# Tables, projections and u in the order of the source: a pipeline over half groups, row tiles of 32 and taps of two terms

## The chip, the core and the metric

The kernel runs on one core of a Trainium2 chip. The metric is the device time of one execution in microseconds (us). Three executions of the kernel before took 1042.09 to 1048.74 us, with a median of 1042.39 us. The core has five engines that each work through a list of instructions of their own in order: PE (matrix multiplication, with weight loads PEld beside it), DVE (vector operations), ACT (activation functions and copies), POOL (vector operations of a second kind) and SP, which here only issues DMAs. An instruction starts when it is first in its engine's list and the semaphores it waits for are there.

## The reference

Two independent computations on inputs of 2048 rows and 576 columns are written side by side into one output of 2048 by 1152.

- Part A is attention. `qkv = x @ wqkv`, 32 heads of 18 columns, a causal window of 256 keys, softmax, and the output projection `@ wo`.
- Part B is a long convolution. For each of 576 channels a kernel of 2048 taps is made from 128 complex modes, `K[d, l] = Re sum_n C[d,n] * exp(dt_d * A[d,n] * l) * dt_d * B[d,n]`. Then `y = u * K` as a causal convolution by transforms of length 4096, plus `u * Dskip`.

## The kernel before

The work runs in three stages.

**Stage 1** makes everything that the second half needs, as three streams that are interleaved in the source by a helper, `merge`, in proportion to their lengths:

- `proj` (line 182) loads x and wqkv, finds a scale for each from their largest absolute values (`amax`, `pow2_scale`), splits both into two float16 halves, and multiplies. `mm14` (line 164) is one group of 14 matmuls of 512 or 288 columns into one PSUM tile. For each of four column chunks of 512 there are nine such groups for q and k, whose results are split again into two float16 halves (`qst`, lines 236 and 237) and stored to DRAM, and four pairs of groups for v (line 248).
- `tables` (line 430) makes the taps of the convolution. The 576 channels come in 36 half groups of 16, and two half groups `c` make a group `q`. The tap at position `l = 64 * a + m` is a product of a coarse factor (over `a`) and a fine one (over `m`). `factors(q)` (line 352) makes the coarse factors of a group: a small matmul, a fraction (ACT line 324, DVE lines 325 and 326), two sines (ACT line 331), then six POOL operations (lines 362 to 373). `products(c)` (line 377) multiplies out two tiles of 128x1024 per half group on POOL (line 384). `phases(c)` and `qtable(c)` make the fine factors: a matmul, a fraction, two sines into PSUM and four DVE products into the tile `Q` (lines 404 to 407). Exponentials for four half groups at a time come from `exps_ab` and `exps_q` (two and eight ACT operations on line 331 from small matmuls on line 314); exponentials and sines need different tables in ACT, so each such block stands between two table loads. `taps(c)` (line 411) sums over the 128 modes: for 4 channels times 4 strips there are four matmuls each (two product tiles, two signs) of 128x32 weights and 64 columns. The profile has two records for each float32 matmul, so one half group has 128 records on line 422.
- `s1_u` (line 470) makes the first step of the transform of u: 32 point transforms over strips of 32 partitions, by a weight of 128x128 that holds the same 32x32 cosine (or sine) block four times on its diagonal (`w1`). Results go to the DRAM tile `gx`.

The order of the instructions of this stage on each engine is set by the framework's scheduler, which reorders the traced instructions by its own cost estimates.

**Stage 2**, `s1_k` (line 479), does for the taps `K` what `s1_u` does for u, and stores them into `gk`. It needs all taps. Beside it the setup of the attention runs (`att_setup`, line 588), with memory fills of the buffers for q and k (lines 601, 603, 604).

**Stage 3** is the attention with the rest of the convolution woven in (`attention`, `conv`), and then the output projection. Its order is already that of the source: it is traced under `manual_schedule()`.

Tile pools set how far the streams can run ahead: a tile with `bufs` buffers can be written again only when all users of the one `bufs` before it are done.

## Time and profile before

| what | value |
|---|---|
| executions, median of 3 | 1042.39 us |
| profiled execution | 1041.77 us |
| its span from first to last instruction | 1040.1 us |
| PE busy | 842.3 us (81%) |
| DVE busy | 703.1 us (68%) |
| POOL busy | 593.5 us (57%) |
| ACT busy | 569.9 us (55%) |
| HBM traffic | 89.12 MB read, 61.01 MB written |

A row of the timeline has the start, the duration, the engine, the line, the operation, the tile written and the tiles read, and in brackets the idle time of the engine before it with what ended the wait. A row of groups has the count after the `x`, then the total busy time and the mean duration in ns, then the idle time before these instructions. A row of stretches has the busy time of PE, PEld, DVE, ACT and POOL, the number of instructions in brackets, the granted clock of PE, the busy share of the DMA engines and GB/s. Busy time is a share of the whole span only as an average; the stretches below show that the three stages are limited by different things.

### The profile page before, as it was taken

Reading aid. Unit: us, or ns where it says so; the run is one execution under the profiler, and the core shown is the slowest. Engines: PE = TensorE matmul, PEld = TensorE weight load, DVE = VectorE, ACT = ScalarE, POOL = GpSimd, SP = SyncE. Lnnn points to the kernel's source line nnn. Section 1 sums busy time; section 2 is a strip of 40 time slices with the busy share of each in tenths; the row PEclk is TensorE's granted clock in tenths of the full one; section 3 lists DMA queues with packets and bytes.
Section 4 is the critical chain, followed back from the end, with each engine's and each line's share of the span. In section 5 each row is a group of like instructions: output and inputs, shape, how many; then the busy total and the mean of one; then the engine's idle time right before and its main releaser. Section 6 shows DMA issues by size and latency. Waiting matters only on the chain.

```text
span 1040.1 us, 26776 instructions
## 1 busy us (share of the span) xinstructions
PE 842.3 (81%) x10332; PEld 443.0 (43%) x10332; DVE 703.1 (68%) x1805; ACT 569.9 (55%) x883; POOL 593.5 (57%) x714
## 2 busy tenths in 40 slices
PE   1433998989799899865788888878888999987787
PEld 0212456446457457532343333333333444433345
DVE  2879374674765675464867788878878676767554
ACT  1784466666666666331266565556666565634470
POOL 0036495674676596301266776757776757664780
PEclk9956899999999999898899999999999999989999
DMA  9655544443454333587144465464544563579863
GB/s 271 182 169 154 133 108 102 113 99 84 124 114 106 79 89 92 135 257 218 48 126 136 130 209 157 147 177 129 158 124 146 144 184 113 152 175 240 222 185 124
DMA packets 155911, 152.27 MB, mean 146 GB/s; under 512 B 36856, under 2 KB 134392, under 8 KB 155592
## 3 DMA queue, kind: packets, MB, share of 16 engines
q1 hardware_dynamic: 148152, 131.98, 46.8%
q0 software_dynamic: 6128, 14.60, 5.5%
q10 hardware_dynamic: 1504, 3.99, 1.4%
q8 instruction: 81, 1.33, 0.6%
q14 instruction: 46, 0.38, 0.1%
HBM read 89.12 MB, written 61.01 MB: 144 GB/s over the span
## 4 chain that ended last, share of the span: by engine, by line
PE 40%; DVE 21%; DMA 12%; issue 10%; ACT 7%; POOL 7%; SPq 2%; DVEq 0%; ACTq 0%; POOLq 0%
PE pp L172 11%; PE r L641 4%; PE kp L422 4%; PE r L505 4%; PE po L705 4%; PE r L908 4%; DVE jk L648 3%; PE pp L466 3%; POOL P L693 3%; PE x L314 2%; DMA gk<-g 2%; PE ST L682 2%; DVE qb L632 2%; ACT P L684 2%; PE r L513 2%
## 5 line engine op out<-in xcount | busy, mean ns | idle before, releaser
L648 DVE CUSTOM_DVE_ANT_0 jk<-r,bias 128x288 f32<-128x288 f32 (+7 forms) x512 | 198.4, 433 | 96.8 <-PE r L641 95.9
L684 ACT ACTIVATE P<-ST,esc 128x1024 f32<-128x1024 f32 (+1 forms) x192 | 201.8, 1058 | 94.5 <-PE ST L682 93.5
L693 POOL TENSOR_SCALAR_AFFINE_SELECT P<-P 128x512 f32<-128x512 f32 x240 | 171.1, 741 | 107.0 <-ACT P L684 104.6
L384 POOL TENSOR_TENSOR m<-A,tr 128x1024 f32<-128x1024 f32 x72 | 145.6, 2045 | 86.8 <-PE kp L422 79.6
L641 PE MATMUL r<-K,qb 128*64 128x288 f16 (+7 forms) x1024 | 130.4, 297 | 38.3 <-DVE qb L632 11.2
L541 POOL TENSOR_TENSOR Y<-t,t 64x288 f32<-64x288 f32 x64 | 52.9, 826 | 119.8 <-DMA tk<-gk 59.8
L705 PE MATMUL po<-P,V 128*32 128x256 f32 (+2 forms) x1408 | 100.6, 397 | 16.9 <-ACT osb L713 8.1
L641 PEld LDWEIGHTS <-qb 128*64 128x64 f16 x1024 | 60.1, 109 | 121.3 <-issue 67.3
L422 PE MATMUL kp<-Q,m 128*32 128x64 f32 x4608 | 80.6, 224 | 16.5 <-issue 6.1
L422 PEld LDWEIGHTS kp<-Q,m 128*32 128x32 f32 x4608 | 70.4, 112 | 38.8 <-issue 26.6
L466 PE MATMUL pp<-ut,w 128*128 128x288 f32 x128 | 47.8, 506 | 42.6 <-DMA ut<-in_u_dram 25.4
L682 PE MATMUL ST<-Q,K 64*128 64x384 f16 (+2 forms) x704 | 73.8, 281 | 3.0 <-DMA Q<-mt 2.9
L325 DVE TENSOR_TENSOR k<-x,k 128x512 f32<-128x512 f32 (+1 forms) x54 | 33.9, 638 | 39.1 <-ACT k L324 39.0
L237 DVE SCALAR_TENSOR_TENSOR qst<-pp,qst 128x512 f16<-128x512 f32 x36 | 24.7, 685 | 50.6 <-ACT qst L236 42.4
L705 PEld LDWEIGHTS po<-P,V 128*32 128x32 f32 x1408 | 35.8, 110 | 51.4 <-issue 26.4
L542 POOL TENSOR_TENSOR Y<-t,t 64x288 f32<-64x288 f32 x64 | 54.4, 851 | 3.8
L172 PE MATMUL pp<-xh,wh 128*128 128x512 f16 x180 | 48.3, 391 | 9.4 <-DVE xh L229 6.5
L128 ACT ACTIVATE g<-pp 128x288 f32<-128x288 f32 (+1 forms) x84 | 34.1, 447 | 37.9 <-DMA gk<-g 20.0
L362 POOL TENSOR_TENSOR tr<-tr,mab 128x768 f32<-128x768 f32 x18 | 34.7, 1929 | 31.1 <-ACT tr L331 31.1
L466 PEld LDWEIGHTS pp<-ut,w 128*128 128x128 f32 x128 | 26.5, 227 | 58.2 <-ACT g L128 17.5
L172 PEld LDWEIGHTS <-wh 128*128 128x128 f16 x324 | 31.6, 99 | 45.7 <-issue 12.4
L505 PE MATMUL r<-tx,w 128*64 128x288 f32 x256 | 41.2, 439 | 10.7 <-DMA tx<-gx 9.5
(173 smaller groups left out, 1755.4 us busy)
## 6 DMA issues: line engine op xcount, KB each, us to landing
gx<-g SPq DMA_DIRECT2D x32, 288.0 KB
qd<-qst SPq DMA_DIRECT2D x72, 128.0 KB
gk<-g SPq DMA_DIRECT2D x16, 576.0 KB
tx<-gx SPq DMA_DIRECT2D x16, 576.0 KB
tk<-gk SPq DMA_DIRECT2D x16, 576.0 KB
h<-ho SPq DMA_DIRECT2D x16, 576.0 KB
raw<-in_xT_dram SPq DMA_DIRECT2D x16, 512.0 KB
Q<-qd SPq DMA_DIRECT2D x32, 216.0 KB
```

What stands on the lines that cost most here:

```text
L172: self.nc.tensor.matmul(ps, u, v, start=(i == 0), stop=(i == len(ops) - 1))
L384: self.nc.gpsimd.tensor_tensor(m, A[:, ch, a0:a0 + 8].unsqueeze(3).to_broadcast(sh), tr[:, ch, part, 0:8].unsqueeze(2).to_broadcast(sh), o ...
L422: nc.tensor.matmul(kp[32 * st:32 * st + 32, c % 2 * JJ2 + j, :], m[:, ch, a0:a0 + 32], Q[:, ch, term % 2, :], start=(term == 0), stop=(ter ...
L466: nc.tensor.matmul(ps, self.w1[:, part, :], src[:, o:o + k], start=True, stop=True)
L505: nc.tensor.matmul(ps[64 * par:64 * par + 64], w2[:, par, 64 * part:64 * part + 64], t[:, 2 * hs:2 * hs + 2, par, :], start=True, stop=True)
L542: nc.gpsimd.tensor_tensor(Y[par][64:128], t1[sl, 1], t2[sl, 1], op=OP.add)
L641: nc.tensor.matmul(ps[64 * b:64 * b + 64, :n], self.qb[:, b, t, :], d["K"][:, b, k0:k0 + n], start=True, stop=True, skip_group_check=True)
L648: nc.vector.tensor_tensor_reduce(out=jk[:, :n], in0=ps[:, :n], in1=self.bias[:, 288 - n:], scale=1.0, scalar=-3e38, op0=OP.add, op1=OP.max ...
L682: nc.tensor.matmul(ps[:, u, o:o + n], d["K"][h, jp, k0:k0 + 128], d["Q"][h, jp, q0:q0 + n], start=True, stop=True, skip_group_check=True)
L684: nc.scalar.activation(pt[:, 2 * jp:2 * jp + 2, lo:hi], ps[:, :, lo:hi], AF.Exp, scale=self.esc)
L693: nc.gpsimd.affine_select(v, v, pattern=[[0, 4], [sg, 128]], compare_op=OP.is_ge, fill=0.0, base=-1 if far else 0, channel_multiplier=-sg)
L705: nc.tensor.matmul(self.po[32 * j:32 * j + 32, t0 * 128:t1 * 128], V[:, kb * 76 + 19 * j:kb * 76 + 19 * j + 32], pt[:, j, o:o + (t1 - t0) ...
```

## The change

Six edits go together.

1. The second `merge` of stage 1 is traced under `manual_schedule()`. On every engine its instructions now stand in the order in which the source emits them. The first, shorter `merge` (16 units of `proj`, 20 of `tables`, 4 of `s1_u`) is still scheduled by the framework.
2. `tables` is written as a pipeline over half groups. In iteration `c` stand: the sum of the two product tiles of `c`, the phases of `c + 2`, the sines and `Q` of `c + 1`, the products of `c + 1`, the first step of the factors of the next group, the taps of `c`, the rest of the factors, and after every fourth the block of exponentials.
3. Taps have two terms. A new step, `sums`, adds the two product tiles on DVE (128x1024), and the taps need two matmuls where they needed four. The pool of the products is split into one with two buffers and one with one.
4. `s1` uses row tiles of 32: the weight is 32x64 (cosine beside sine), and each of the four strips is multiplied by itself into 64 PSUM partitions. `gx` and `gk` are laid out with the strip as an index, each store becomes four of 64 partitions where two of 128 partitions stood, `s1_k` has 16 steps of 4 rows where 8 of 8 rows stood, and `conv` loads `tx` and `tk` in two halves each.
5. The loads of x for the projections and of u are issued one chunk earlier.
6. Three pairs of fills with zero in the attention's setup (line 603) are left out.

```diff
 def proj:
+        load(0)
         for c in range(4):
...
             for hf in range(2):
-                t = self.p["raw"].tile([128, 5, 256], F32, name="raw")
-                self.load_rows(t, a["xT"], slice(c * 512 + hf * 256, c * 512 + hf * 256 + 256))
+                t = raws.pop(0)
...
+                if m == 1 and c < 3:
+                    load(c + 1)

 def products:
-            m = self.p["P"].tile(sh, F32, name="m%d" % part)
+            m = self.p["P%d" % part].tile(sh, F32, name="m%d" % part)
+    def sums(self, c):
+        r = self.P[c]
+        self.nc.vector.tensor_tensor(r[0], r[0], r[1], op=OP.add)
+        self.P[c] = r[0].rearrange("p c a b -> p c (a b)")

 def taps:
         for j in range(JJ2):
-            for term in range(4):
-                m = (m1, m2)[term // 2]
-                a0 = term % 2 * 32
+            for term in range(2):
                 for st in range(4):
                     ch = st * JJ2 + j
-                    nc.tensor.matmul(kp[32 * st:32 * st + 32, c % 2 * JJ2 + j, :], m[:, ch, a0:a0 + 32],
-                                     Q[:, ch, term % 2, :], start=(term == 0), stop=(term == 3), skip_group_check=True)
+                    nc.tensor.matmul(kp[32 * st:32 * st + 32, c % 2 * JJ2 + j, :], P[:, ch, 32 * term:32 * term + 32],
+                                     Q[:, ch, term, :], start=(term == 0), stop=(term == 1), skip_group_check=True)

 def tables:
-        for c in range(n):
-            if c % 2 == 0 and c // 2 + 1 < NQ:
-                yield from self.factors(c // 2 + 1)
-            if c + 1 < n:
-                self.phases(c + 1)
-                yield
-            yield from self.qtable(c)
-            yield
-            if c % 4 == 3 and c + 1 < n:
-                if c + 5 < n:
-                    yield from self.exps_ab(c // 4 + 2)
-                yield from self.exps_q(c // 4 + 1)
-            if c:
-                yield from self.taps(c - 1)
-            if c + 1 < n:
-                self.products(c + 1)
-        yield from self.taps(n - 1)
+        for c in range(-1, n):
+            if c >= 0:
+                self.sums(c)
+            if c + 2 < n:
+                self.phases(c + 2)
+                yield
+            if c + 1 < n:
+                yield from self.qtable(c + 1)
+                if c >= 0:
+                    self.products(c + 1)
+                yield
+            fa = self.factors(c // 2 + 1) if c % 2 == 0 and c + 2 < n else iter(())
+            if next(fa, 0) is None:
+                yield
+            if c >= 0:
+                yield from self.taps(c)
+            yield from fa
+            if (c + 1) % 4 == 3 and c + 2 < n:
+                if c + 6 < n:
+                    yield from self.exps_ab((c + 1) // 4 + 2)
+                yield from self.exps_q((c + 1) // 4 + 1)

 def s1:
+        st = [self.p["s1s"].tile([128, n], F32, name="g%d" % e) for e in range(2)]
+        for o in range(0, n, k):
+            ps = [self.p[pp].tile([128, 512], F32, name="pp")[:, :k] for _ in range(2)]
+            for q in range(4):
+                r, h = slice(32 * q, 32 * q + 32), 64 * (q % 2)
+                nc.tensor.matmul(ps[q // 2][h:h + 64], self.w1[r], src[r, o:o + k], start=True, stop=True,
+                                 skip_group_check=True)
+            for e in range(2):
+                self.evac(st[e][:, o:o + k], ps[e])
+        for q in range(4):
+            h = 64 * (q % 2)
+            nc.sync.dma_start(g[l0:l0 + nl, q].rearrange("l p j -> p l j"),
+                              st[q // 2][h:h + 64].rearrange("p (l j) -> p l j", j=144))

 def s1_k:
-        for b in range(8):
-            self.s1(kf[:, b * 1152:(b + 1) * 1152], self.gk, 8 * b, 8, "s1p")
+        for b in range(16):
+            self.s1(kf[:, b * 576:(b + 1) * 576], self.gk, 4 * b, 4, "s1p")

 def conv:
-                nc.sync.dma_start(t[nm], g.rearrange("a l (s f) j -> (a l) s f j", s=4)[:, :, 2 * fp:2 * fp + 2, :])
+                for e in range(2):
+                    f0 = 32 * e + 2 * fp
+                    nc.sync.dma_start(t[nm][64 * e:64 * e + 64], g[:, :, f0:f0 + 2])

 def att_setup:
-                nc.vector.memset(d["K"][h:h + 32], 0.0)

 def build:
-                                 ("mg", 4), ("fr", 2), ("Q", 2), ("P", 2)):
+                                 ("mg", 4), ("fr", 2), ("Q", 2), ("P0", 2), ("P1", 1)):
-                    merge((proj, 56), (tables, 304), (s1u, 12))
+                    with self.tc.manual_schedule():
+                        merge((proj, 56), (tables, 304), (s1u, 12))
-                    self.pool(e1, "s1p", 3, PSUM)
+                    self.pool(e1, "s1p", 4, PSUM)
```

38 lines of the change are left out of this document (19 added, 19 removed).

## The prediction

> **What bounds the kernel now.** I read the stretches first, to see which of the three stages the change touches and what each costs.
>
> ```profile
> 0.00:106.00 106.00, 36.83 (x339) 19.45 (x340) 73.94 (x82) 56.89 (x71) 27.51 (x26) 0.79 0.67 190
> 106.00:428.00 322.00, 297.69 (x5510) 184.15 (x5510) 191.45 (x284) 198.12 (x355) 210.73 (x168) 0.98 0.44 105
> 428.00:479.00 51.00, 36.74 (x108) 18.02 (x100) 30.03 (x29) 17.16 (x37) 2.40 (x1) 0.94 0.76 223
> 479.00:1041.00 562.00, 471.08 (x4386) 221.41 (x4386) 407.67 (x1412) 297.71 (x421) 352.88 (x520) 0.97 0.55 155
> ```
>
> Stage 1 runs to 428 us. From 106 us on, when the first projection starts, PE is busy in 298 of 322 us, DVE, ACT and POOL in 191 to 211. So PE sets the pace there, and the scheduler keeps it fed. Stage 2 (51 us) has the DMA engines at 0.76. Stage 3 (562 us) is touched only through how two tiles are loaded.
>
> Next the groups of stage 1 and single pieces of the timeline:
>
> ```profile
> L384 POOL TENSOR_TENSOR m<-A,tr 128x1024 f32<-128x1024 f32 x72 | 145.6, 2045 | 86.8 <-PE kp L422 79.6 <-issue 7.2
> L331 ACT ACTIVATE mg<-x 128x512 f32<-128x512 f32 x72 | 40.1, 599 | 8.8 <-PE x L314 8.3
> L325 DVE TENSOR_TENSOR k<-x,k 128x512 f32<-128x512 f32 x36 | 24.6, 682 | 2.7 <-ACT k L324 2.6
> L404 DVE TENSOR_TENSOR Q<-cs,mg 128x512 f32<-128x512 f32 x36 | 24.6, 684 | 3.0 <-ACT cs L331 3.0
> L261 DVE TENSOR_TENSOR res<-nA_re,al 96x2304 f32<-96x2304 f32 x1 | 2.5, 2547 | 0.0
> ...
> 300.23 1.03 PE L172 MATMUL pp<-xl,wh 128*128 128x512 f16 x4
> 301.18 1.99 PE L422 MATMUL kp<-Q,m 128*32 128x64 f32 x128
> ```
>
> One half group's taps take PE 1.99 us. Products are a slack engine's work: POOL idled 79.6 us before them, waiting for the taps that still read the old buffers.
>
> **The change, part by part.** *Taps of two terms* remove half of 1.99 us for each of the some 34 half groups after 106 us: 34 us of PE. *The sums* come to DVE: 2304 columns of two SBUF inputs took 2547 ns, so 1024 take 1.13 us, 34 x 1.13 = 38 us. DVE goes from 191 to about 230 of 322 us if nothing disturbs it. *Row tiles* can shorten PE by up to half of each pass over u, if the four strips run side by side. Attention's row tiles bear on that:
>
> ```profile
> 709.76 0.39 PE L682 MATMUL ST<-Q,K 64*128 64x384 f16 x4
> 710.08 0.50 PE L641 MATMUL r<-K,qb 128*64 128x288 f16 x4
> ```
>
> Four matmuls of 384 columns on two row halves took 0.32 us until the next started. In the fence above, the float16 group starts four of 512 columns in 0.95 us (300.23 to 301.18), 0.18 us per 384: one after another, four would need 0.71 us. So two row tiles do run side by side. By loads alone PE falls from 298 to about 255 us, and the stage ought to shrink.
>
> **But the new order decides what replaces PE.** In the manual order each engine keeps the source's order, so the waits can be walked through. I do this for a period of four half groups, the distance between two blocks of exponentials. These are the period's marks before (table loads of ACT) and one complete passage through the factors:
>
> ```profile
> 153.35 1.28 ACT L331 ACT_TABLE_LOAD   x1
> 169.59 1.28 ACT L331 ACT_TABLE_LOAD   x1 [0.18 <-DVE k L325]
> ...
> 388.44 1.28 ACT L331 ACT_TABLE_LOAD   x1
> ...
> 269.48 0.56 DVE L325 TENSOR_TENSOR k<-x,k 128x384 f32<-128x384 f32 x1
> 270.07 0.36 DVE L326 TENSOR_SCALAR ab<-k 128x384 int32<-128x384 int32 x1
> 270.13 0.52 ACT L331 ACTIVATE tr<-k 128x384 f32<-128x384 f32 x1 [7.18 <-DVE k L325]
> 270.56 0.60 ACT L331 ACTIVATE tr<-ab,halfpi 128x384 f32<-128x384 f32 x1
> 271.30 1.81 POOL L362 TENSOR_TENSOR tr<-tr,mab 128x768 f32<-128x768 f32 x1 [3.44 <-ACT tr L331]
> 276.21 3.86 POOL L384 TENSOR_TENSOR m<-A,tr 128x1024 f32<-128x1024 f32 x2
> ...
> 306.32 0.58 ACT L331 ACTIVATE sn<-k 128x512 f32<-128x512 f32 x1
> 306.84 0.67 ACT L331 ACTIVATE cs<-ab,halfpi 128x512 f32<-128x512 f32 x1
> ...
> 195.89 0.87 ACT L331 ACTIVATE mab<-x 128x384 f32<-128x384 f32 x2
> ...
> 156.95 2.24 ACT L331 ACTIVATE mg<-x 128x512 f32<-128x512 f32 x4
> ```
>
> From the load at 153.35 to that at 388.44 lie six periods, so one is 39.2 us now.
>
> In the new source, DVE does for half group c: sums(c), the phases' two operations, four products into Q(c+1), and for even c the factors' two operations. Those factors are first used by products(c+2), and sums(c+2) stands first in iteration c+2. So there is only one half group's DVE work between a fraction and the sum that waits for it through ACT and six plus two POOL operations. By the fence, that passage takes 280.07 - 269.48 = 10.6 us. Then follow on DVE, in order, the sum 1.13, phases 0.6 and 0.35, and Q at 4 x 0.6 (0.68 each, overlapping a little) = 2.4, with handovers 15.2 us until the next even half group's fraction. This is a closed chain over two half groups that no relief of PE shortens. The other two half groups contain the exponentials: ACT reaches them only after the sines of the factors (tr), so after the same DVE work, and the next Q needs them. That chain is: table 1.28, sines 1.2, Q 2.5; one half group of DVE 4.7; the pair above 15.2; from the fraction to the end of tr 1.7 (269.48 to 271.16); table 1.28; two operations mab 0.9; eight mg at 0.56 = 4.5; one fraction copy 0.6. **The bare period is 33.9 us.**
>
> Loads on this chain, from both sides (nothing, or as follows):
>
> ```profile
> L326 DVE TENSOR_SCALAR ab<-k x54: 342/467/2150, 68.4 to 416.2; 128x512 int32<-128x512 int32 x36, 128x384 int32<-128x384 int32 x18
> L384 POOL TENSOR_TENSOR m<-A,tr x72: 1941/1955/3827, 78.2 to 419.2; 128x1024 f32<-128x1024 f32 x72
> L764 DVE TENSOR_TENSOR osb<-osb,spread x28: 681/1124/1290, 561.8 to 990.5; 128x512 f32<-128x512 f32 x28
> ...
> L237 DVE SCALAR_TENSOR_TENSOR qst<-pp,qst 128x512 f16<-128x512 f32 x36 | 24.7, 685 | 50.6 <-ACT qst L236 42.4 <-DMA qd<-qst 7.1 <-DMA gx<-g 1.2
> ```
>
> The same operation takes 0.34 or 2.15 us on DVE, and 1.94 or 3.83 us on POOL: each sometimes waits for about one whole operation of the other. In the new order this is systematic: the end of sums(c) releases the second product of c+1 on POOL, and 0.6 us later DVE comes to the `ab` operation, 1.95 - 0.6 = 1.3 us before POOL is done. That is 1.3 us in two of the four half groups on the chain = 2.6, and a sum that falls into the factors delays POOL by 1.1. Next, three evictions of projections (`qst`, 0.685 each) stand in DVE's list in the chain: 2.0. In the exponentials ACT also evicts projections and u (1.2 us), and PE has a whole group of 14 matmuls (14 x 0.24 = 3.3 us by the fence) between two of the small ones with two PSUM buffers, where the scheduler had placed single matmuls: 2.6 after the 0.7 us that buffered work covers. Sum 9.5, **so the loaded period is 43.4 us.** Some of this falls into slack; the loads are nearer to certain than to absent, since each follows from the order, and I take four fifths: 33.9 + 7.6 = **41.5 us, 2.3 more than now.**
>
> The Trainium skill, page "SBUF — State Buffer", section "Who interferes with whom", has the rule that a DVE instruction with two SBUF inputs, or in a two-port mode, and a GpSimd instruction that reads SBUF share a port pair whose loser fully blocks. This trace agrees (1.3 to 1.9 us of wait on 0.34 and 1.95 us operations). Without such blocking the loaded period would be some 39.7 us, which is the period of now.
>
> *Start.* POOL changes over between products and the scale's reduction:
>
> ```profile
> 92.72 1.96 POOL L384 TENSOR_TENSOR m<-A,tr 128x1024 f32<-128x1024 f32 x1
> 100.72 0.38 POOL L144 PARTITION_ALL_REDUCE xg<-xm  x1 [6.04 <-PE x L314]
> 108.28 1.94 POOL L384 TENSOR_TENSOR m<-A,tr 128x1024 f32<-128x1024 f32 x1 [7.18 <-issue]
> ```
>
> It loses 6.0 + 7.2 us around it. The built order of POOL places only two half groups' products and one group's factors ahead of this, where three half groups and two groups stood; the second factors come behind it, and on DVE behind the casts of x. So the tables' pipeline starts later by the factors and up to one half group: between 0 and 14 us. I take 10. The first projection itself stays at 106 us, since the same scale and casts release it.
>
> *Prefetch of x and u.* Nothing: PE's work is no longer what is late, and the casts stand at their old place in DVE's list. *Tail:* +2, as the last half groups run in the longer period.
>
> *Stage 2.*
>
> ```profile
> ACT g L128 <- DMA gk<-g: 20.0, 11, 3.0
> L603 DVE MEMSET K<- 32x1280 uint32 x6 | 6.8, 1125 | 1.6 <-issue 1.6
> ...
> 428.41 1.03 ACT L428 ACTIVATE K<-kp 128x512 f32<-128x512 f32 x1 [7.02 <-PE kp L422]
> 434.26 2.38 SPq L468 DMA_DIRECT2D gk<-g  x2
> 438.69 0.37 SPq L468 DMA_DIRECT2D gk<-g  x1
> 478.95 0.57 SPq L496 DMA_DIRECT2D tx<-gx  x1
> ```
>
> Evictions wait for stores here (20.0 us), and bytes stay the same. Steps of half the size let the first store start after half of the work (428.4 to 434.3 us before), -2.5; 6.8 us less of fills, of which I count 1.5. Together -4. Sixty-four issues instead of 16 cost SP about 0.4 us each, 26 of 51 us, which the stores' own time covers. If not covered, +5.
>
> *Stage 3.* 32 more issues at 0.57 us lie half a frequency pair ahead of use: 0; uncovered once, at the start, +1.
>
> *Sum.* Start +10, seven periods at +2.3 = +16, tail +2, stage 2 -4: +24. The profiled execution took 1041.8 us (0.6 us below the median of the three): **1066 us.**
>
> **Rivals.**
>
> *The chain runs bare and PE's relief is what shows (faster).* For it: 34 us less on PE, and PE at 92% before. If evictions and port waits fall into slack, the period is 35.2 (bare plus half the exponentials' stall): 7 x -4.0 = -28, start +5, tail -3, stage 2 -4, so 1012 us; reaching up to 1030. It decides where the period is below 38.1 us (7 x -1.1 pays for start and tail). Against it: it needs DVE to run nearly without a wait.
>
> *No change.* The scheduler's period and the source's are alike, 38 to 39 us, and the start costs what stage 2 gives: 1042 us.
>
> *Row tiles run one after another, so the change doesn't do what it says there.* Each pass is then 4 x 288 float32 columns where it was 2 x 288. From 428 to 479 PE was busy 36.7 us: it would become about 60 us, more than the stores, +12. With the full 43.4 us period (7 x 4.2 = +29), start +14 and tail +4: 1101 us. The row above with two tiles side by side speaks against it. The Trainium skill, "TensorEngine Tiling (Array Packing)", section "Restrictions and Gotchas", says different row tiles cannot access the same PSUM bank simultaneously; here strips 0 and 1 share a bank, so by that page at most two of the four run together. No row here has two row tiles in one bank.
>
> **How the numbers follow.** The forecast of a slower kernel has 0.45, the serial or fully loaded case 0.10, no change 0.17, the faster case 0.28. The range goes from 1008 us (the faster case nearly whole) to 1096 (just short of the slowest). Slower by over 1% takes the first two, 0.55; 1% is about what a measurement of this kernel can tell from no change.
>
> **What would show it.** In the profile after: distance between every second table load (41.5 forecast, under 38.1 for the faster case); idle time of DVE before the sums, released by POOL's products; `ab` operations near 1.7 us; PE's busy time in stage 1 about 255 us with gaps before the taps, released by the sums; first-step matmuls of stage 2 overlapping four at a time. I am wrong if DVE never waits for POOL, or if the exponentials' block takes under 9 us.

## The result, and the profile after

The changed kernel took 1147.15 us (median of four executions, 1140.16 to 1149.94), beside 1044.56 us for the kernel before (1042.09 to 1048.74). The ratio is 1.0968, 95% interval 1.0901 to 1.1034: slower, as forecast, but by 103 us where 24 were forecast, and outside the range.

The stretches of the profile after (us, busy time of PE, PE's loads, DVE, ACT and POOL with their instructions, granted clock, DMA share, GB/s):

```profile
0.00:106.00 106.00, 26.72 (x93) 7.62 (x93) 64.73 (x62) 45.82 (x51) 18.52 (x19) 1.00 0.65 181
106.00:520.00 414.00, 307.48 (x3581) 161.60 (x3581) 276.87 (x341) 208.97 (x376) 222.99 (x175) 0.85 0.36 83
520.00:591.00 71.00, 38.25 (x258) 14.58 (x260) 22.95 (x26) 18.81 (x49) 0.95 (x1) 0.60 0.81 188
591.00:1147.00 556.00, 472.89 (x4386) 221.33 (x4382) 407.12 (x1412) 298.40 (x421) 354.27 (x520) 0.96 0.59 153
```

Stage 1 from 106 us on is 414 us long where it was 322. PE executes some 1900 matmuls fewer there (5510 to 3581) and is still busy 307 us (298 before), at a granted clock of 0.85 instead of 0.98. DVE is busy 277 us instead of 191. No engine is near full any more. Stage 2 has grown too (the table below counts both alike), stage 3 is as before.

ACT's timeline, the table loads ahead of the exponentials (the first, second and last of eight), and its last eviction of the table K:

```profile
132.71 1.28 ACT L338 ACT_TABLE_LOAD   x1
...
178.61 1.28 ACT L338 ACT_TABLE_LOAD   x1
...
476.90 1.28 ACT L338 ACT_TABLE_LOAD   x1
...
519.52 1.02 ACT L439 ACTIVATE K<-kp 128x512 f32<-128x512 f32 x1 [10.79 <-PE kp L433]
```

With the first matmul of stage 3 (at 590.66, below; 484.36 before) these marks divide the 107.0 us by which the profiled span grew (1040.1 to 1147.1):

| part | before | after | growth | forecast |
|---|---|---|---|---|
| to the first block of exponentials | 114.2 (worked out: 153.35 less one period of 39.2) | 132.71 | +18.5 | +10 |
| seven periods | 39.2 each | 49.2 each (476.90 - 132.71 = 344.2, by 7) | +70 | +16 |
| last block to the last eviction of K | 40.0 | 42.6 | +2.6 | +2 |
| stage 2, to the first matmul of stage 3 | 55.9 | 71.1 | +15.2 | -4 |
| stage 3 | 555.7 | 556.4 | +0.7 | 0 |

Below, "period" is always this mean of seven distances between the table loads ahead of the first and of the eighth block. For the kernel before it is the mean of the last six, as in the prediction, since its first block stands ahead of its first projection (105.79):

```profile
100.54 1.28 ACT L331 ACT_TABLE_LOAD   x1
```

From there to the second block at 153.35 lie 52.8 us, which hold part of the start; with them the mean would be 41.1. So start and period can be parted otherwise than in the table: from second block to second block +25.3 us (153.35 to 178.61), then six periods of 39.2 before and 49.7 after, +63. Two pairs of runs that differ only in their stores show how well a period repeats: 49.2 and 49.7, 38.5 and 38.8. Stage 3, which none of the experiments touches, took 548.7 to 557.5 us.

The longest sums of waits in the seven periods (who waited for what: us in total, times, longest):

```profile
POOL tr L369 <- ACT tr L338: 73.7, 15, 6.7
ACT tr L338 <- DVE k L332: 59.2, 12, 10.2
POOL m L392 <- DVE m L399: 58.4, 19, 11.8
ACT qst L241 <- PE pp L169: 53.5, 15, 12.6
DVE qst L242 <- ACT qst L241: 52.5, 12, 8.9
...
PE kp L433 <- DVE m L399: 40.1, 12, 6.1
```

Every engine waits for every other. PE, which hardly waited before, stands 40 us ahead of the taps until DVE's sum is there. DVE waits mostly in line, at `qst`, the projections' evictions, and for POOL's products only 11.8 us, as the groups of the same stretch show (busy us, mean ns | idle before):

```profile
L399 DVE TENSOR_TENSOR m<-m,m 128x1024 f32<-128x1024 f32 x28 | 49.7, 1776 | 11.9 <-POOL m L392 11.8
L169 PE MATMUL pp<-xh,wl 128*128 128x512 f16 x160 | 46.3, 426 | 0.0
L333 DVE TENSOR_SCALAR ab<-k 128x512 int32<-128x512 int32 (+1 forms) x42 | 46.1, 1098 | 1.4
L433 PE MATMUL kp<-Q,m 128*32 128x64 f32 x1792 | 38.3, 246 | 40.7 <-DVE m L399 40.1 <-ACT cs L338 0.3 <-ACT qst L241 0.3
```

A sum takes 1.78 us in the mean, where the prediction had 1.13 us from an operation beside which POOL was idle. The mean hides two cases (durations of all 36 sums, ns minimum/median/maximum, then a sum with POOL idle and one beside POOL's products):

```profile
L399 DVE TENSOR_TENSOR m<-m,m x36: 1209/1260/2962, 92.5 to 516.2; 128x1024 f32<-128x1024 f32 x36
...
150.26 1.21 DVE L399 TENSOR_TENSOR m<-m,m 128x1024 f32<-128x1024 f32 x1
...
464.57 3.86 POOL L392 TENSOR_TENSOR m<-A,tr 128x1024 f32<-128x1024 f32 x2
466.56 2.96 DVE L399 TENSOR_TENSOR m<-m,m 128x1024 f32<-128x1024 f32 x1 [3.52 <-POOL m L392]
```

Ten of the 36 sums ran with no POOL operation beside them, and each took 1.21 to 1.23 us. The longest come just behind the start of the second product, and last until 1.09 us after its end (466.56 + 2.96 = 469.52, the product ends at 468.43). So DVE's waits for POOL are the 11.8 us above and, inside the sums' own durations, some 0.55 us each.

One turn of the circle, from the timeline of all engines:

```profile
255.38 1.84 DVE L399 TENSOR_TENSOR m<-m,m 128x1024 f32<-128x1024 f32 x1
...
257.27 1.93 PE L433 MATMUL kp<-Q,m 128*32 128x64 f32 x64 [5.32 <-DVE m L399]
...
259.14 2.31 PE L169 MATMUL pp<-xh,wh 128*128 128x512 f16 x5
...
261.24 1.29 PE L169 MATMUL pp<-xh,wl 128*128 128x512 f16 x5
...
262.38 1.03 PE L169 MATMUL pp<-xl,wh 128*128 128x512 f16 x4
...
263.49 0.60 ACT L241 ACTIVATE qst<-pp 128x512 f16<-128x512 f32 x1 [7.16 <-issue]
263.98 1.03 ACT L439 ACTIVATE K<-kp 128x512 f32<-128x512 f32 x1
264.12 0.69 DVE L242 SCALAR_TENSOR_TENSOR qst<-pp,qst 128x512 f16<-128x512 f32 x1 [3.14 <-ACT qst L241]
264.73 2.03 DVE L399 TENSOR_TENSOR m<-m,m 128x1024 f32<-128x1024 f32 x1
```

PE stands 5.3 us until the sum is there. After that gap its taps and the first five matmuls of the projection behind them run slowly: 2.31 us for these five, 1.29 us for the next five; the granted clock is 0.50 from 254.5 to 261.3. ACT stands 7.2 us in line for this group of 14 (its row names no releaser, but the group's last matmul ends at 263.41, just ahead of ACT's start), DVE 3.1 us for ACT, and behind that on DVE stands the next sum.

### The profile page after: what moved, and what is told of

Its sections match the earlier page's. It is cut to its first block, busy times and chain, and to the rows that moved or that the text cites. A ratio compares the mean times of both kernels' runs of the same rounds, so it can differ in the third digit from the quotient of the medians.

```text
span 1147.1 us, 22897 instructions
## 1 busy us (share of the span) xinstructions
PE 845.3 (74%) x8316; PEld 405.1 (35%) x8316; DVE 771.7 (67%) x1839; ACT 572.0 (50%) x895; POOL 596.7 (52%) x714
## 4 chain that ended last, share of the span: by engine, by line
PE 28%; DVE 25%; issue 11%; DMA 11%; POOL 9%; ACT 9%; SPq 6%; DVEq 0%; ACTq 0%; POOLq 0%
PE pp L169 6%; PE r L536 4%; PE r L671 4%; PE r L938 3%; PE po L735 3%; DVE m L399 3%; DVE jk L678 2%; POOL P L723 2%; PE ST L712 2%; SPq L490 2%; PE pp L484 2%; POOL m L392 2%; DMA w<-in_c_w_dram 2%; PE r L544 2%; DVE osb L794 1%
## 5 line engine op out<-in xcount | busy, mean ns | idle before, releaser
L392 POOL TENSOR_TENSOR m<-A,tr 128x1024 f32<-128x1024 f32 x72 | 142.0, 1984 | 108.1 <-DVE m L399 68.2
L572 POOL TENSOR_TENSOR Y<-t,t 64x288 f32<-64x288 f32 x64 | 53.5, 836 | 135.8 <-DVE t L567 133.8
L484 PE MATMUL pp<-ut,w 32*64 32x288 f32 x256 | 44.4, 553 | 86.4 <-ACT g L125 67.2
L433 PE MATMUL kp<-Q,m 128*32 128x64 f32 x2304 | 50.0, 248 | 55.6 <-DVE m L399 54.9
L399 DVE TENSOR_TENSOR m<-m,m 128x1024 f32<-128x1024 f32 x36 | 63.4, 1762 | 16.0 <-POOL m L392 15.9
L433 PEld LDWEIGHTS kp<-Q,m 128*32 128x32 f32 x2304 | 42.4, 128 | 74.2 <-DVE m L399 31.3
L241 ACT ACTIVATE qst<-pp 128x512 f16<-128x512 f32 x36 | 21.3, 592 | 87.3 <-PE pp L169 69.1
L536 PE MATMUL r<-tx,w 128*64 128x288 f32 x256 | 42.1, 446 | 27.8 <-DMA tx<-gx 26.7
L169 PE MATMUL pp<-xh,wh 128*128 128x512 f16 x180 | 59.1, 470 | 4.1 <-DVE xh L234 4.1
L333 DVE TENSOR_SCALAR ab<-k 128x512 int32<-128x512 int32 (+1 forms) x54 | 56.7, 1051 | 1.8
L332 DVE TENSOR_TENSOR k<-x,k 128x512 f32<-128x512 f32 (+1 forms) x54 | 34.2, 636 | 34.0 <-ACT k L331 33.7
L484 PEld LDWEIGHTS pp<-ut,w 32*64 32x64 f32 x256 | 14.2, 160 | 112.8 <-ACT g L125 78.5
```

Of the source, the lines that this page charges most:

```text
L169: self.nc.tensor.matmul(ps, u, v, start=(i == 0), stop=(i == len(ops) - 1))
L392: self.nc.gpsimd.tensor_tensor(m, A[:, ch, a0:a0 + 8].unsqueeze(3).to_broadcast(sh), tr[:, ch, part, 0:8].unsqueeze(2).to_broadcast(sh), o ...
L399: self.nc.vector.tensor_tensor(r[0], r[0], r[1], op=OP.add)
L433: nc.tensor.matmul(kp[32 * st:32 * st + 32, c % 2 * JJ2 + j, :], P[:, ch, 32 * term:32 * term + 32], Q[:, ch, term, :], start=(term == 0), ...
L484: nc.tensor.matmul(ps[q // 2][h:h + 64], self.w1[r], src[r, o:o + k], start=True, stop=True, skip_group_check=True)
L536: nc.tensor.matmul(ps[64 * par:64 * par + 64], w2[:, par, 64 * part:64 * part + 64], t[:, 2 * hs:2 * hs + 2, par, :], start=True, stop=True)
```

## The experiments

All ratios are to the kernel before on the same chip, with their 95% intervals. The first three groups take stage 1 apart, the fourth stage 2.

### Order, sums and short taps

**The scheduler instead of the source's order.**

```diff
-                    with self.tc.manual_schedule():
-                        merge((proj, 56), (tables, 304), (s1u, 12))
+                    merge((proj, 56), (tables, 304), (s1u, 12))
```

> The changed kernel, but stage 1 is placed by the scheduler again instead of in the order of the source; sums, taps of two terms, row tiles and the new source stay. Three theories for the 70 us that seven periods between blocks of exponentials gained (49.2 us each instead of 39.2). ORDER: a fixed order in which each engine waits in line for work that it could have overtaken; then the period falls back to between 36 and 40 us, the granted clock in stage 1 back above 0.95, and the time is 1147 minus 63 to 92, and minus up to 18 at the start: 1045 to 1085 us. SUMS: one more DVE operation for each half group, with its waits for POOL, is what lengthens the period; then the period stays at 46 us or more and the time above 1120 us. ROW TILES in u's passes: likewise unchanged, above 1130 us. Stage 2 is expected to keep its 70 us under each.

Measured: 1.0559 (1.0503 to 1.0614), 1099.5 us; period 44.7 us.

```profile
120.17 1.28 ACT L338 ACT_TABLE_LOAD   x1
...
432.93 1.28 ACT L338 ACT_TABLE_LOAD   x1
```

Neither theory alone: the order costs 4.5 us of the 10, and 5.5 us stay without it (6.6 and 4.0 over the last six distances). The scheduler's placing has a wait of its own, DVE's for POOL's products ahead of the sums in the seven periods, 75 us where the order has 11.9:

```profile
L399 DVE TENSOR_TENSOR m<-m,m 128x1024 f32<-128x1024 f32 x29 | 51.3, 1769 | 75.0 <-POOL m L392 75.0
```

**The order alone, in the kernel before.** The same two lines, the other way, in the old source.

> The kernel before, with nothing changed but that stage 1 after its first part runs in the order of its (old) source: four-term taps, no sums, no row tiles, old prefetch. ORDER: the period between blocks of exponentials grows from 39.2 to between 43 and 50 us, the granted clock falls below 0.93, the time is 1075 to 1120 us. SUMS or ROW TILES: nothing of theirs is in this kernel, so the time is that of before within 1%, 1034 to 1055 us.

Measured: 1.1316 (1.1267 to 1.1365), 1177.2 us; period 55.2 us. That is beyond even the range of ORDER. Without a sum, a short tap or a row tile, running the old source in its order costs more than the whole change. The change's new source is thus much the better one to run in order, and still not good enough.

**Four-term taps, no sums, in order.**

```diff
-            if c >= 0:
-                self.sums(c)
...
-            for term in range(2):
+            for term in range(4):
```

> The changed kernel in the order of its source, but with taps of four terms and no sums (both product tiles get two buffers, u's row tiles stage one buffer less to make room). DVE loses 36 operations of 1.76 us mean (63 us), PE gains 36 times 1 us, and taps wait for the products themselves. SUMS: the period falls by at least 5 us and the time to 1085 to 1115 us. CHAIN: two of the four sums of a period and their handover leave the chain, 2 to 4 us of 49.2, so 1118 to 1135 us. IN-LINE EVICTIONS: PE's groups move apart by 1 us in each half group while the waits for sums go: 1130 to 1165 us.

Measured: 1.0605 (1.0548 to 1.0663), 1105.1 us; period 44.2 us, from 128.51 to 437.73. The case SUMS: 5.0 us of a period, though PE has 4 us more to do.

**The same under the scheduler**, which closes the square.

> Four-term taps and no sums, as in the run with four terms, but placed by the scheduler; row tiles, half fills and the new source stay. It closes a square: order or scheduler, with or without sums; so far the period is 49.2 (order, sums), 44.2 (order, none), 44.7 us (scheduler, sums). ADDITIVE (each of the two costs some 5 us of a period by itself): 39 to 40 us here and 1055 to 1072 us, the rest above before being stage 2's 15 us. ROW TILES cost stage 1 something too: 41 us or more and above 1075 us. SHARED (one wait which either of the two removes): 44 us, 1090 to 1100 us.

Measured: 1.0072 (1.0039 to 1.0105), 1049.8 us; period 38.5 us.

```profile
120.39 1.28 ACT L338 ACT_TABLE_LOAD   x1
...
389.96 1.28 ACT L338 ACT_TABLE_LOAD   x1
```

ADDITIVE, and a little better than that: row tiles, prefetch and new source cost the periods nothing (over the same six distances 37.5 us against 39.2 before). In this square, which changes sums and taps together, the two costs stand side by side; with the taps kept short they do not quite (the table below).

**No sums, but short taps, in order.** Taps read the first products alone.

> The changed kernel in the order of its source with taps of two terms, but the sums are left out: taps read the first products alone, the second products are computed and never used. So PE has the short taps, and DVE has no sums. DVE WAITS (the sums lengthen the period by their time, their port waits and the wait of the taps for them): the period is 44.2 us as with four terms or up to 4 us less, as PE's relief shows: 40 to 44.5 us, and the time 1080 to 1106 us. CLOCK (PE, relieved, runs at a lower granted clock, and its groups of 14 take longer by what the taps save): the period stays at 47 to 49 us at a granted clock of 0.80 to 0.86 and the time at 1130 to 1148 us.

Measured: 1.0467 (1.0413 to 1.0522), 1090.0 us; period 43.7 us, from 123.21 to 429.20. So DVE WAITS. PE's relief of 4 us a period is worth 0.5 us in the order (44.2 to 43.7), no more than a period repeats to. Nobody reads the second products here, so POOL's buffer for them is never held; this run takes that wait away together with the sums.

**Four-term taps and sums, in order.**

> Four-term taps in the order of the source with the sums added as well: each sum overwrites the first products, and the taps then take four terms of both tiles (so the values differ from the reference's). PE is loaded as with four terms, DVE as in the changed kernel. DVE WAITS: the period is 49 to 53 us, that of the changed kernel or up to 4 us more, the time 1145 to 1180 us. CLOCK: with PE busy again the clock is at 0.90 or above and the period 44 to 46 us, the time 1100 to 1120 us.

Measured: 1.1073 (1.103 to 1.1115), 1154.8 us; period 50.2 us at a granted clock of 0.88 in it. DVE WAITS again: 6.0 us for the sums with long taps, 5.5 with short ones. It is not the clock that parts them: it is 0.88 in the run before this one too, whose period is 6.5 us shorter.

**No sums, short taps, under the scheduler.**

> The changed kernel with taps of two terms on the first products alone (the sums and the second products' part of the taps are left out), placed by the scheduler. With four terms and no sums the scheduler's period is 38.5 us and the time 1049.8 us. PE SETS THE PACE: four half groups lose 1 us of PE each, the period falls to 34.5 to 36.5 us and the time to 1022 to 1037 us. ANOTHER CHAIN sets it as well (POOL and ACT for the factors, ACT for exponentials and evictions): 37.5 to 39 us and 1042 to 1054 us.

Measured: 0.9867 (0.982 to 0.9913), 1027.0 us; period 35.6 us (118.36 to 367.42). PE SETS THE PACE where it is fed: 2.9 of the 4 us come through. (Here too the second products are never read, and how much of the 2.9 us is due to that was not tried.) Together these runs take the period apart (in brackets over the last six distances):

| period, us | four terms, no sums | two terms, no sums | two terms, sums |
|---|---|---|---|
| scheduler | 38.5 (37.5) | 35.6 (35.0) | 44.7 (43.2) |
| order of the source | 44.2 (44.9) | 43.7 (44.4) | 49.2 (49.7) |

Along the upper row and down: short taps -2.9, sums +9.1, order +4.5. Down first: order +8.1, sums +5.5. So with short taps the two costs overlap: together they make 13.6 us, where each alone makes 9.1 and 8.1. Whichever way one walks, the sums cost more than the short taps save.

### What of a sum costs

**An addition that nobody waits for.**

```diff
+                self.nc.vector.tensor_tensor(junk, junk, junk, op=OP.add)
-                self.sums(c)
```

> The kernel without sums (two-term taps on the first products alone, in the order of the source), with an addition of the sums' size, two SBUF inputs of 1024 columns, at the place of each sum, but on a tile that nobody else reads or writes (s1's staging tile has one buffer less to make room). DVE thus spends the time and meets POOL at its port, but no engine waits for the result. Periods so far: 49.2 us with sums, 43.7 us without. DVE TIME: 48 to 50 us, 1125 to 1150 us. HANDOVER (what costs is that DVE waits for the product and taps wait for the sum): 43.5 to 45 us, 1085 to 1102 us.

**A sum of 16 columns.**

```diff
-        self.nc.vector.tensor_tensor(r[0], r[0], r[1], op=OP.add)
+        t = [z[:, :, 0, 0:1] for z in r]
+        self.nc.vector.tensor_tensor(t[0], t[0], t[1], op=OP.add)
```

> The changed kernel with each sum cut down to one column of 16 elements per partition (the rest of the second products is left out of the taps): POOL's products, DVE and the taps wait for each other at the same places as in the changed kernel, but DVE spends next to nothing on the sum. HANDOVER: the period is 48 to 50 us, the time 1125 to 1150 us. DVE TIME (with the port that it shares with POOL): 43.5 to 45 us and 1085 to 1102 us. If both this run and the one with the idle addition come out between, each has its part.

Measured: 1.0744 (1.0702 to 1.0787) and 1.0707 (1.0653 to 1.0761); 1120.9 and 1118.3 us; periods 46.0 (131.65 to 453.45) and 46.4 us (128.24 to 453.09). Both lie between 43.7 and 49.2, +2.3 and +2.7, which make 5.0 of the 5.5 us: each has its part. (The run with the idle addition has one staging buffer less for u, which no run tried by itself.) The additions in the two profiles, the idle one first:

```profile
L456 DVE TENSOR_TENSOR junk<-junk 128x1024 f32<-128x1024 f32 x36 | 62.9, 1748 | 0.1
```

```profile
L400 DVE TENSOR_TENSOR m<-m,m 128x16 f32<-128x16 f32 x36 | 24.1, 671 | 15.0 <-POOL m L392 14.9
```

The idle addition waits for nobody's result and still takes 1.75 us, so this time is not the handover's. Sixteen columns take 0.67 us in the mean: 0.18 to 0.20 us in the 17 cases with POOL idle, and up to 1.92 us beside a product. So this run did not take away all of DVE's time, and its 2.7 us hold some of that beside the wait. The Trainium skill ("SBUF — State Buffer", "Who interferes with whom") has two-input DVE operations and POOL's reads lock each other out. These rows agree with it, as do the prediction's and the sums' 1.21 us with POOL idle against up to 2.96 us: whatever its size, the addition waits for the rest of the product.

### What of the order costs

**Factors one half group earlier.**

```diff
-            fa = self.factors(c // 2 + 1) if c % 2 == 0 and c + 2 < n else iter(())
+            fa = self.factors((c + 3) // 2) if c % 2 and c + 3 < n else iter(())
```

> The changed kernel, still in the order of its source, but the factors of a pair of half groups are issued one half group earlier, so two half groups of DVE work instead of one lie between a fraction and the sum that waits for it through ACT and eight POOL operations. CHAIN (the prediction's: the period is the closed chain fraction, sines, POOL, sum): the period falls from 49.2 to 40 to 44 us and the time to 1090 to 1115 us. IN-LINE EVICTIONS (a rival: ACT and DVE wait in line for the groups of 14 matmuls that they evict, and PE in line for the sums, so every wait is passed on): the chain has no slack to give, the period stays within 1.5 us and the time within 1136 to 1158 us. SUMS: likewise unchanged.

Measured: 1.087 (1.0812 to 1.0927), 1129.3 us; period 48.7 us. Of the 18 us (10 by the ratios, each to the kernel before on its own chip) 11.6 come from the start (first block at 121.10 instead of 132.71) and little from the period, which moved by 0.5 us (by 1.4 over the last six distances). The prediction's closed chain does not set it.

**Evictions one projection later.**

```diff
-                nc.scalar.activation(st[:, 0], ps, AF.Copy, scale=S)
...
+                self.flush()
+                self.late.append(evict)
```

> The changed kernel in the order of its source, but each projection's evictions (ACT, DVE, its stores) are issued one unit of projections later, when the next group of 14 matmuls stands already in PE's line; sums and short taps stay. IN-LINE EVICTIONS (a circle over three in-order lists: taps wait on PE for a sum, the group of 14 behind them is late, ACT and DVE wait in line for that group, and the next sum stands behind that wait on DVE): the waits of ACT for PE's groups (69 us now) fall below 25 us and the period from 49.2 to 43 to 46 us, the time to 1105 to 1130 us. CHAIN or DVE TIME: these waits were slack; the period stays within 1.5 us and the time within 1136 to 1158 us.

Measured: 1.0951 (1.0904 to 1.0998), 1140.6 us; period 49.0 us. The waits that were aimed at did go: ACT's at `qst` for PE's groups is no longer listed, DVE's for ACT at `qst` fell from 52.5 to 35.7 us. But POOL's wait for buffers that taps still read rose from 31.3 to 46.6 us and DVE's for ACT's fractions (`k`) from 33.7 to 53.5, and the period stayed. In-line evictions were where the wait was seen, not its cause.

**The exponentials in one piece,** with sums and without:

```diff
-                    yield from self.exps_ab((c + 1) // 4 + 2)
-                yield from self.exps_q((c + 1) // 4 + 1)
+                    for _ in self.exps_ab((c + 1) // 4 + 2):
+                        pass
+                for _ in self.exps_q((c + 1) // 4 + 1):
+                    pass
+                yield
...
-                        merge((proj, 56), (tables, 304), (s1u, 12))
+                        merge((proj, 56), (tables, 234), (s1u, 12))
```

> The changed kernel in the order of its source, but the ten small products and exponentials of a block are issued one behind the other, with no projection and no pass over u between them (the number of steps by which projections are spread is set to the new count). From the table load of the exponentials to the next one it takes 14.1 us now. BLOCK (that is where the order loses against the scheduler): the block falls to 8 to 10 us, the period from 49.2 to 44 to 46 us, the time to 1110 to 1128 us. ELSEWHERE (the groups of 14 that stood inside now stand before the taps instead): the block shortens as well, but the rest of the period grows by as much; the period stays at 47.5 to 50 us, the time at 1135 to 1155 us.

> The same in the kernel with four-term taps and no sums, in the order of its source (44.2 us period, 1105 us). BLOCK: the period falls to 39 to 41 us, near the scheduler's 38.5, and the time to 1070 to 1085 us. ELSEWHERE: 43 to 45 us and 1096 to 1112 us.

Measured: 1.0808 (1.078 to 1.0836), 1126.2 us, period 46.3 us; and 1.0711 (1.0679 to 1.0744), 1114.5 us, period 45.2 us. The block fell to 10.3 and 10.2 us in the mean, nearly as far as wanted, but the period fell by 2.9 us in the one and rose by 1.0 us in the other. The first lies between the two cases, nearer to BLOCK, the second with ELSEWHERE: the wait is seen in the block, but shortening the block alone is not a cure.

**Three edits together,** on four-term taps: earlier factors, later evictions, exponentials in one piece.

> Four-term taps without sums in the order of the source, with three edits together: factors one half group earlier, evictions of projections one unit later, exponentials in one piece. Alone they moved a period by -0.5 and -0.2 us (with sums) and by +1.0 us (without). SEVERAL WAITS: together they give more than their sum, 39 to 42 us a period against 44.2, and 1066 to 1092 us. Otherwise (these three are not where the order loses): 43 to 46 us and 1095 to 1120 us.

Measured: 1.0612 (1.055 to 1.0674), 1108.6 us; period 44.0 us. They give nothing together either.

**Groups of 14 matmuls cut into five, five and four,** without sums and with:

```diff
             self.nc.tensor.matmul(ps, u, v, start=(i == 0), stop=(i == len(ops) - 1))
+            if i in (4, 9):
+                yield
...
-                        merge((proj, 56), (tables, 304), (s1u, 12))
+                        merge((proj, 192), (tables, 304), (s1u, 12))
```

> Four-term taps without sums in the order of the source, with each group of 14 matmuls cut into pieces of five, five and four between which the source order may place the tables' work (projections are spread by their new number of steps). PIECES: the tables' small products no longer wait for whole groups; the period falls from 44.2 to 39.5 to 42 us, towards the scheduler's 38.5, and the time to 1068 to 1092 us. SEVERAL WAITS: the group ends later for the evictions that wait in line for it, and the period stays at 43 to 46 us, the time at 1096 to 1120 us.

> The changed kernel with its groups of 14 matmuls cut in the same way. PIECES: the period falls from 49.2 to 44 to 47 us, the time to 1105 to 1132 us. SEVERAL WAITS: 48 to 50 us and 1138 to 1155 us.

Measured: 1.0347 (1.0285 to 1.0409), 1081.6 us; and 1.0768 (1.0704 to 1.0832), 1123.5 us. The two table loads of each, without sums first:

```profile
131.25 1.28 ACT L340 ACT_TABLE_LOAD   x1
...
417.23 1.28 ACT L340 ACT_TABLE_LOAD   x1
```

```profile
134.03 1.28 ACT L340 ACT_TABLE_LOAD   x1
...
458.98 1.28 ACT L340 ACT_TABLE_LOAD   x1
```

The periods are 40.9 and 46.4 us: PIECES, -3.3 of the 5.7 us that the order costs without sums and -2.8 of 4.5 with them. This is the one edit that helps both. What the remaining 2.4 and 1.7 us are stays open (3.7 and 3.3 over the last six distances).

### Stage 2

In the profile after, the last stage before the attention: SP's timeline with the first matmul that reads its result, and the durations of its store issues (ns minimum/median/maximum).

```profile
523.26 46.27 SPq L490 DMA_DIRECT2D gk<-g  x64
...
570.72 0.36 SPq L651 DMA_DIRECT2D K<-qd  x1
...
578.20 1.95 SPq L527 DMA_DIRECT2D tx<-gx  x2
```

```profile
590.66 2.19 PE L536 MATMUL r<-tx,w 128*64 128x288 f32 x8 [26.65 <-DMA tx<-gx]
```

```profile
L490 SPq DMA_DIRECT2D gk<-g x64: 574/614/1788, 523.3 to 568.9; - x64
```

The first store came 3.7 us after K's last eviction started (5.9 before), as forecast. But SP issues without a break: 46.27 us for 64 stores of 64 partitions, 0.72 each. The seven loads of Q and K, which stood between the stores before, come behind them, and the first matmul waits 26.7 us for `tx`.

**Stores of 128 partitions.** Same bytes, same places.

```diff
-        for q in range(4):
-            h = 64 * (q % 2)
-            nc.sync.dma_start(g[l0:l0 + nl, q].rearrange("l p j -> p l j"),
-                              st[q // 2][h:h + 64].rearrange("p (l j) -> p l j", j=144))
+        for e in range(2):
+            nc.sync.dma_start(g[l0:l0 + nl, 2 * e:2 * e + 2].rearrange("l q p j -> (q p) l j"),
+                              st[e].rearrange("p (l j) -> p l j", j=144))
```

> The changed kernel with each staging tile of the first step stored by one transfer of 128 partitions and 288 KB instead of two of 64 partitions and 144 KB; destinations, bytes and runs of 576 bytes are the same, loads are untouched. HEIGHT OR NUMBER OF TRANSFERS (stage 2's stores moved 191 to 206 GB/s, 239 to 248 before): the store phase falls from 46.3 us to 37 to 41 us and the time by 6 to 10 us, 1137 to 1141 us. If instead SP's QUEUE (loads of Q and K behind all stores) is the whole of stage 2's 15 us: the store phase keeps 44 to 47 us and the time stays within 3 us of the changed kernel's.

Measured: 1.0883 (1.0836 to 1.093), 1134.2 us, 13 us less than the changed kernel (9 by the ratios, each to the kernel before on its own chip). Issues, rate, and the last eviction of K and the first matmul of stage 3 in this run:

```profile
L489 SPq DMA_DIRECT2D gk<-g x32: 359/362/491, 527.9 to 571.8; - x32
...
528.00:572.00 44.00, 34.21 (x238) 14.38 (x232) 21.02 (x24) 17.33 (x45) 0.00 (x0) 0.66 0.83 238
...
524.15 1.03 ACT L439 ACTIVATE K<-kp 128x512 f32<-128x512 f32 x1 [10.78 <-PE kp L433]
...
582.05 2.19 PE L535 MATMUL r<-tx,w 128*64 128x288 f32 x8 [12.34 <-DMA tx<-gx]
```

For comparison a stretch of 15 us amid the stores of the changed kernel, and one of the kernel before:

```profile
535.00:550.00 15.00, 14.19 (x84) 5.07 (x84) 8.12 (x9) 5.41 (x15) 0.00 (x0) 0.50 0.82 191
```

```profile
445.00:460.00 15.00, 11.08 (x32) 5.34 (x31) 9.67 (x10) 4.85 (x11) 0.00 (x0) 1.00 0.87 248
```

From K to the first matmul 57.9 us remain of 71.1 (55.9 before). Neither case came as written. The store phase kept its 44 us, as the QUEUE case had it, but the time fell by more than the other case gave, since seven loads of Q and K now fit between the stores. An issue of half the height and half the bytes costs SP more, 0.61 us against 0.36 us, and the rate goes from 191 back to 238 GB/s. More than SP's list changed: by the traces' DMA records a packet of 576 bytes took 39.0 ns in the mean during the changed kernel's stores, 32.2 in this run and 31.8 in the kernel before.

The Trainium skill has a rule that speaks of this: "SBUF — State Buffer", "Door 1: The DMA port swizzle (why `[64,N]` ≈ `[32,N]`)", says that a transfer's bandwidth depends on how many of SBUF's ports its partitions reach, and that 64 partitions of one half reach eight of the sixteen; it gives 196 GB/s for partitions 0 to 63, measured at 1 MiB. The changed kernel's stores, at 191 GB/s in the stretch above and 206 from 550 to 569 us, lie near it; this run changed number and height together and does not part them.

### A version that is faster than both

The run with four-term taps under the scheduler, with the stores of 128 partitions:

> Row tiles, half fills, the new source and the early loads of the change, with four-term taps, no sums, placed by the scheduler (period 38.5 us before against 39.2), and with the first step's stores of 128 partitions (13 us in the changed kernel). The sum of the parts: 1049.8 - 13 = 1037 us, 0.994 of the kernel before; between 0.985 and 1.003.

Measured: 0.9949 (0.9926 to 0.9972), 1037.7 us, period 38.8 us. The change without its order, its sums and its short taps, and with full-height stores, is 0.5% faster than the kernel before; that is little, but the interval excludes 1.

## Why the prediction was wrong in size

The sign was right, for reasons that were right in part. By its own steps:

- **PE sets the pace of stage 1.** Right: under the scheduler 2.9 of 4 us come through when taps are halved. That PE would fall to about 255 us was wrong: 307 us, at a lower granted clock, with gaps before the taps as foretold.
- **The sums, 1.13 us each, 38 us of DVE.** Mis-sized: 1.76 us, 63 us in all, of which 1.21 us each is the sum by itself and the rest the wait for POOL. Of a period's four sums the sum of terms counted two and their knock on POOL, 3.4 us with the handovers aside, and it hung 2.6 us of `ab` on the sums' ends too: 6.0 us in full. The runs give 5.5 and 6.0 us in the order and 9.1 under the scheduler. So in the order the sums cost about what was charged for them, though not along this chain, and that is more than all that the short taps could give (4 us).
- **The closed chain through the factors, bare 33.9 us.** This step failed as a mechanism. With the factors a half group earlier the period moved by 0.5 us; DVE waited 12 us in all seven periods for POOL's products. In its place the runs show what the order costs without any sum: 43.7 us in the order against 35.6 under the scheduler, 8.1 us, where the chain without the terms of the sums would be some 36 us (41.5 less 2.3 and four fifths of 3.7). I walked one loop through the lists and took all others for loads of that loop. The term for PE's groups of 14, 2.6 us, had the right object in the wrong place: it was charged once, in the exponentials. Cutting the groups gave 2.8 to 3.3 us, and the exponentials' block alone did not explain it.
- **The period, 41.5 us.** Measured 49.2. Even all loads in full gave 43.4: the range had no case in which order and sums both cost this much.
- **`ab` near 1.7 us, exponentials over 9 us.** Right in kind: the 512-column `ab` operations took 1.4 us in the mean, the block 14.1 us. The 0.34 us that the prediction set beside 2.15 is the 384-column form's; with 512 columns the shortest took 0.41 us.
- **Start +10, first projection at 106 us.** Measured +18.5; the first projection came at 110.9 us. Earlier factors alone took 11.6 us of it back (121.10). That fits the step's reason, second factors that come too late, but does not show it: in that run the scale's reduction on POOL also came 10.9 us earlier (90.97 instead of 101.82). The bounds, 0 to 14, were too narrow; the 18.5 us rest on the worked-out mark of 114.2.
- **Stage 2, -4.** Failed: +15.2. The term was 64 issues at 0.4 us, covered by the stores' own time, or else +5. An issue took 0.61 us, with its waits 0.72, so SP's list was 46 us long with the loads of Q and K behind it; and the step took bytes alone for the price of a transfer. With full-height stores +2.0 is left.
- **Tail +2, stage 3 nothing.** Right: +2.6, +0.7.
- **Row tiles side by side.** Right, in full. The passes over u, a row of before and one after:

```profile
203.95 2.21 PE L466 MATMUL pp<-ut,w 128*128 128x288 f32 x8
```

```profile
272.88 0.71 PE L484 MATMUL pp<-ut,w 32*64 32x288 f32 x8
```

Full-height matmuls start 0.26 us apart ((2.21 - 0.40) / 7, one taking 0.40). Eight in two steps of four end after 0.26 + 0.40 = 0.66 us, in four steps of two after 3 x 0.26 + 0.40 = 1.18 us. Measured 0.71 (the end is modelled): four together, two and two of them in one bank. In the trace's records the first four start within 0.02 us of each other, the other four 0.29 us later. The rule of the Trainium skill that the prediction weighed ("TensorEngine Tiling (Array Packing)", "Restrictions and Gotchas") does not hold here for two row tiles that write different halves of a bank's partitions, and the rival of serial row tiles falls.

The rivals "faster" and "no change" needed a period below 39.2 us, which only runs without the sums and without the order showed.

## What to carry to other kernels

Before work is moved from the engine that is the bound to one with slack, count what it does to the handovers: here an operation of 1.2 us on DVE, between POOL and PE, cost more of the period than the microsecond of PE that it saved. An order written out by hand loses what a scheduler gains by splitting long groups of matmuls, here some 3 us of a period; cut the groups before the order is judged, and judge the order by itself. A store's price is not its bytes: here transfers of all 128 partitions went faster, and the issues on the queue that others share had to be counted.

## What the runs showed of the hardware unexpectedly

- An issue of a store of 64 partitions and 144 KB occupied SP for 0.61 us, one of 128 partitions and 288 KB for 0.36 us (medians of 64 and of 32 issues in stage 2).
- A busier PE did not mean a higher granted clock. In the two stretches of stage 2 above PE was busy 14.19 of 15 us after, with matmuls of 32 rows, at 0.50, and 11.08 of 15 us before, with matmuls of 128 rows, at 1.00. The rows alone do not decide it: from 523 to 535 us the same matmuls of 32 rows had 0.93, with PE busy 8.83 of 12 us. What decides it, and what it would cost where such tiles are the bound, was not tried.
- An addition on DVE took 1.21 us with POOL idle and up to 2.96 us beside a product of POOL (16 columns: 0.18 and up to 1.92 us). The wait stands inside the duration, not in the idle time before it.
- Two row tiles that wrote different partitions of one PSUM bank ran at the same time (0.71 us for eight, above).
